# A fused attention and token-mixing kernel: band mask moved to TensorE, coarse rows carried through their own projections, two PSUM slot sizes, TensorE kept in traced order

## The chip, the cores and the metric

The kernel runs on one core of one Trainium2 chip. Times are device microseconds (us) of one execution. A span is the time from the first to the last instruction of one profiled execution. It lies about 2 us under the time of the same execution. PE is TensorE, DVE VectorE, ACT ScalarE, POOL GpSimd, SP the engine whose queue issues most of the DMAs.

The kernel before shows two levels in its runs, near 246 and near 250 us. Runs more than 1.5% above the fastest of the same kernel are called slow and are left out of every ratio.

The profile of the kernel before is of an execution of 249.87 us, on the upper level (1.6% above the fastest run, so slow by the rule above). No profile of the lower level was kept.

## The reference

```python
# q, k, v: 8 batches x 8 heads x 576 rows x 64, float32
out_d    = softmax_attention(mean4(q), mean4(k), mean4(v))   # 144 coarse rows per head
out_up   = np.repeat(out_d, 4, axis=2)                       # back to 576 rows
mask     = np.abs(pos[:, None] - pos[None, :]) < 4           # a band of 7
out_loc  = softmax_attention(q, k, v, masked with mask)
x        = (out_up + out_loc) as [8, 576, 512]
wq, wk   = x @ w_q, x @ w_k                                  # 64 wide each
W        = (wq @ wk.T) / 8
out      = np.maximum(W @ x, 0) @ w_out                      # [8, 576, 512]
```

## The kernel before

Each batch passes through four stages. `stage_cast` loads a batch and casts it on POOL. `stage_a` transposes q and k on PE, sums groups of four rows on POOL, computes the local scores in windows of 58 queries by 64 keys, takes exp on ACT, and averages v on PE. `stage_b` does the coarse attention and the local products, and builds x and its transpose. `stage_c` does the mixing. One iteration of the main loop merges `stage_c` of batch i-2, `stage_b` of i-1, `stage_a` of i and the cast of i+1. The parts that the change and the argument touch:

```python
ps2 = tile_pool(name="ps2", bufs=4, space=PSUM)        # four slots of two banks, for everything
# ... masks, averaging matrices P, selection matrices sel: some 70 small POOL instructions ...
merge([stage_cast(0)])                                  # traced behind all of them

def score(pr_):                                         # local scores of one or two windows
    for i, n in enumerate(pr_):
        for hl in range(NP):
            for p, c in ((0, 0), (1, 1), (0, 1), (1, 0)):
                nc.tensor.matmul(p_[64*c:64*c+64, p, o:o+w], kT[...], qT[...], start=True, stop=True, ...)
    nc.scalar.activation(E, p_, Exp, scale=s_local)
    for n, t_ in e_:                                    # the band mask, on DVE
        nc.vector.tensor_tensor(t_, t_, masks[n], op=mult)

def sums():                                             # groups of four rows, on POOL
    # 2 additions of 128x1152, one of 128x576, five small ones: 7.2 us in all

def vd():                                               # averages of v
    # 5 matmuls from v16 into pv; ACT copies vd0, DVE multiplies into vblk

def up(n):                                              # coarse rows added to x
    nc.tensor.matmul(pu[:, 0, :], sel[n], od, start=True, stop=True)
    nc.vector.tensor_tensor(x_, x_, pu[:, 0, :], op=add)

def wt():                                               # wT = [wq wk] transposed
    for i in range(2):
        for r in range(4):
            nc.tensor.matmul(p_[:, i, 0:320], wqk16[:, r, :], xT[:, r, 320*i:320*i+320], ...)
# m2: 5 matmuls wk x; mx(r): four evacuations with ReLU; og(i): output matmuls, evacuation, store
```

The softmax here doesn't subtract the row's maximum and nothing guards it: scores larger than these inputs give would overflow.

Of the kernel before, what the change touches and what calls it, by code (L numbers as in the profile page):

```python
# [17 lines left out]

@with_exitstack
def kernel(  # L20
# [10 lines left out]
    nc = tc.nc  # L31
    B, H, S, D = q.shape
    DM = H * D
# [20 lines left out]
    ps2 = ctx.enter_context(tc.tile_pool(name="ps2", bufs=4, space=bass.MemoryType.PSUM))  # L54

    def ps(dtype=FP32, name="ps"):
        return ps2.tile([128, 2, 512 if dtype == FP32 else 1024], dtype, name=name, tag="ps")

# [41 lines left out]
    masks = {}  # L100
    for n in (0, 1, 4):
        t_ = cst.tile([128, WQ[n]], FP16, name=f"mask{n}")
        nc.vector.memset(t_, 1.0)
        for c in range(2):
            h_, off = t_[64 * c:64 * c + 64], K0[2 * n + c] - Q0[2 * n + c]
            asel(h_, [[-1, WQ[n]]], ALU.is_ge, 0.0, off + 3, 1)
            asel(h_, [[1, WQ[n]]], ALU.is_ge, 0.0, 3 - off, -1)
        masks[n] = t_
    masks[2] = masks[3] = masks[1]


    P = []
    for n in range(NW):
        t_ = cst.tile([128, 32], FP16, name=f"P{n}")
        nc.vector.memset(t_, 0.0)
        mid = (K0[2 * n] + 64) // 4 - G0[n]
        for c, lo, hi in ((0, 0, mid), (1, mid, GN[n])):
            u_ = t_[64 * c:64 * c + 64, lo:hi]
            off = K0[2 * n + c] - 4 * (G0[n] + lo)
            nc.vector.memset(u_, 0.25)  # L120
            asel(u_, [[-4, hi - lo]], ALU.is_ge, 0.0, off, 1)
            asel(u_, [[4, hi - lo]], ALU.is_ge, 0.0, 3 - off, -1)
        P.append(t_)
    P4 = cst.tile([128, 4, 32], FP16, name="P4rep")
    nc.vector.tensor_copy(P4, _ap(P[4], 0, [[row(P[4]), 128], [0, 4], [1, 32]]))
    blk = cst.tile([128, 4], FP16, name="blk")
    nc.vector.memset(blk, 1.0)
    asel(blk, [[-32, 4]], ALU.is_ge, 0.0, 0, 1)
    asel(blk, [[32, 4]], ALU.is_ge, 0.0, 31, -1)


    GR = 116
    sel = []
    for n in range(NW):
        t_ = cst.tile([128, 2, 64], FP16, name=f"sel{n}")
        nc.vector.memset(t_, 0.0)
        for c in range(2):
            u_ = t_[:, c, 0:WQ[n]]
            off = Q0[2 * n + c] - (4 * GR if n == 4 else 0)
            nc.vector.memset(u_, 1.0)  # L140
            asel(u_, [[1, WQ[n]]], ALU.is_ge, 0.0, off, -4)
            asel(u_, [[-1, WQ[n]]], ALU.is_ge, 0.0, 3 - off, 4)
        sel.append(t_.rearrange("p c w -> p (c w)"))


    rows = cst.tile([128, 2], FP32, name="rows")
    nc.vector.memset(rows, 1.0)
    for c in range(2):
        for i, w in ((0, WQ[0]), (1, WQ[4])):
            asel(rows[64 * c:64 * c + 64, i:i + 1], [[0, 1]], ALU.is_ge, 0.0, w - 1, -1)  # L150


    kdS, E_S, vd0S, vblkS, od1S = [], [], [], [], []
    for i in range(2):
        t_ = cst.tile([128, NP, 160], FP16, name=f"kd_{i}")
        nc.vector.memset(t_, 0.0)
        kdS.append(t_)
        es = {}
        for pr_ in PAIRS:
            t_ = cst.tile([128, 2, len(pr_), NP, 64], FP16, name=f"E{pr_[0]}_{i}")  # L160
            nc.vector.memset(t_, 1.0)
            es[pr_] = t_
        E_S.append(es)
        t_ = cst.tile([128, H, 65], FP16, name=f"vd0_{i}")
        nc.vector.memset(t_, 1.0)
        for n in range(4):
            asel(t_[32 * n:32 * n + 32, :, 64], [[0, H]], ALU.is_ge, 0.0, GN[0] - 1, -1)
        vd0S.append(t_)
        t_ = cst.tile([128, 2, 4, 65], FP16, name=f"vblk_{i}")
        nc.vector.memset(t_, 0.0)  # L170
        o_ = t_[:, :, :, 64]
        nc.vector.memset(o_, 1.0)
        asel(o_, [[0, 2], [-32, 4]], ALU.is_ge, 0.0, 0, 1)
        asel(o_, [[0, 2], [32, 4]], ALU.is_ge, 0.0, GN[4] - 1, -1)
        vblkS.append(t_)
        t_ = cst.tile([128, DM], FP16, name=f"od1_{i}")
        nc.vector.memset(t_, 0.0)
        od1S.append(t_)

    nc.vector.tensor_copy(wqk16, w32)  # L180
    for i in range(2):
        nc.vector.tensor_copy(wo16[:, 2 * i:2 * i + 2], wo32[i])
# [3 lines left out]
    def stage_cast(b):  # L186
# [12 lines left out]
        def vv():  # L199
            v32 = g["in"][3]  # L200
            v16 = g["v16"] = big.tile([128, NW, H, 65], FP16, name="v16", tag="v16", bufs=3)
            nc.gpsimd.tensor_copy(v16[:, :, :, 0:64], v32)
            nc.gpsimd.memset(v16[:, :, :, 64:65], 1.0)
# [3 lines left out]
    def stage_a(b):  # L207
        g = st[b]

        def tr(key):  # L210
            def f_():
                t_ = g[key]
                p_ = g["p" + key] = ps(FP16, "p" + key)
                for j in range(NP):
                    for f in range(4):
                        o = (j % 2) * 512 + 128 * f
                        nc.tensor.transpose(p_[:, j // 2, o:o + 128],  # L217
                                            t_[:, f, 2 * j:2 * j + 2, :], id16)
# [9 lines left out]
        def rem():  # L228
            qT, kT = g["qT"], g["kT"]
            pr = ps(FP16, "pr")  # L230
            for j in range(NP):
                nc.tensor.transpose(pr[:, 0, 128 * j:128 * j + 128],
# [25 lines left out]
        def score(pr_):  # L258
            def f_():
# [4 lines left out]
                for i, n in enumerate(pr_):  # L264
                    for hl in range(NP):
                        for p, c in ((0, 0), (1, 1), (0, 1), (1, 0)):
                            m = 2 * n + c
                            o = i * W + hl * w
                            nc.tensor.matmul(p_[64 * c:64 * c + 64, p, o:o + w],  # L269
                                             kT[64 * p:64 * p + 64, hl, K0[m]:K0[m] + 64],  # L270
                                             qT[64 * p:64 * p + 64, hl, Q0[m]:Q0[m] + w],
                                             start=True, stop=True, tile_position=(64 * p, 64 * c))
# [5 lines left out]
                if pr_ == (1, 2):  # L278
                    e_ = [(1, E.rearrange("p a n h w -> p (a n h) w")[:, :, 0:w])]
                else:  # L280
                    e_ = [(n, E[:, :, i, :, 0:w]) for i, n in enumerate(pr_)]
                for n, t_ in e_:
                    m_ = masks[n]
                    bc = [[0, t_.shape[1]]] if len(t_.shape) == 3 else [[0, 2], [0, NP]]
                    nc.vector.tensor_tensor(t_, t_, _ap(m_, 0, [[row(m_), 128]] + bc + [[1, w]]),  # L285
                                            op=ALU.mult)
            return f_

        def vd():
            v16, vd0, vblk = g["v16"], vd0S[b % 2], vblkS[b % 2]  # L290
            pv = ps(name="pv")
            for n in range(4):
                nc.tensor.matmul(pv[32 * n:32 * n + 32, 0, :], P[n], v16[:, n, :, 0:64],
                                 start=True, stop=True, tile_position=(0, 32 * n))
            nc.tensor.matmul(pv[:, 1, :], P4.rearrange("p a t -> p (a t)"), v16[:, 4, :, 0:64],
# [12 lines left out]
    def stage_b(b):  # L308
        g = st[b]
        vd0, vblk, od1 = vd0S[b % 2], vblkS[b % 2], od1S[b % 2]  # L310
# [3 lines left out]
        def cs(i):  # L314
            def f_():
                kd, qd = kdS[b % 2], g["qd"]
                if i == 0:
                    g["Ec"] = big.tile([128, 2, 2, 2, T], FP16, name="Ec", tag="Ec")
                p_ = ps(name="pcs")
                for hh in range(2):  # L320
                    for p in range(2):
                        nc.tensor.matmul(p_[:, p, hh * T:(hh + 1) * T],  # L322
# [3 lines left out]
                nc.scalar.activation(g["Ec"][:, i].rearrange("p a c t -> p a (c t)"),  # L326
                                     p_[:, :, 0:2 * T], ACTF.Exp, scale=s_coarse)
            return f_

        def cr():  # L330
            kd, qd = kdS[b % 2], g["qd"]
            Er = g["Er"] = big.tile([128, 2, T], FP16, name="Er", tag="Er")
            p_ = ps(name="pcr")
            for hl in range(NP):
                for p in range(2):
                    nc.tensor.matmul(p_[32 * hl:32 * hl + 32, p, 0:T],
                                     kd[64 * p:64 * p + 64, hl, 128:160],
                                     qd[64 * p:64 * p + 64, hl, :],
                                     start=True, stop=True, tile_position=(64 * p, 32 * hl))
            nc.scalar.activation(Er, p_[:, :, 0:T], ACTF.Exp, scale=s_coarse)  # L340

        def ca(i):
            def f_():
                Ec, Er = g["Ec"], g["Er"]
                if i == 0:
                    g["od0"] = big.tile([128, DM], FP16, name="od0", tag="od0")
                    g["rc"] = big.tile([128, 2, 2, 4], FP32, name="rc", tag="rc")
                od, rc = (g["od0"], od1)[i], g["rc"]
                lo, hi = ((0, 128), (GR, T))[i]
                M = hi - lo  # L350
                p_ = ps(name="pca")
                for p in range(2):
                    nc.tensor.matmul(p_[0:M, p, 0:260], Er[:, p, lo:hi],  # L353
                                     vblk[:, p].rearrange("a h e -> a (h e)"),
                                     start=True, stop=False, skip_group_check=True)
                    for hl in range(NP):
                        nc.tensor.matmul(p_[0:M, p, 65 * hl:65 * hl + 65],  # L357
                                         Ec[:, hl // 2, p, hl % 2, lo:hi], vd0[:, 2 * hl + p, :],
# [7 lines left out]
            return f_  # L366

        def av(n):
            def f_():
# [6 lines left out]
                for s_ in range(2):  # L376
                    for hh in range(NP):
                        for c in range(2):
                            h = 4 * (s_ ^ c) + hh
                            nc.tensor.matmul(  # L380
# [12 lines left out]
        def up(n):  # L393
            def f_():
                x_ = g["x"][n]
                pu = ps(name="pu")
                nc.tensor.matmul(pu[:, 0, :], sel[n], od1 if n == 4 else g["od0"],
                                 start=True, stop=True)
                nc.vector.tensor_tensor(x_, x_, pu[:, 0, :], op=ALU.add)
            return f_  # L400
# [159 lines left out]
```

## Time and profile before

| | before |
|---|---|
| time, median of three runs | 246.19 us (245.99 to 250.73) |
| span of the profiled execution (249.87 us, upper level) | 248.1 us |
| start of the third batch's sums (filling) | 68.1 us |
| one iteration (see below) | 25.62 us |
| from the eighth batch's sums to the end (draining) | 52.3 us |

The sums of a batch are one easily found POOL instruction per iteration, so their starts serve as a clock. An iteration is a quarter of the time from the fourth batch's sums to the eighth's, by the timeline of POOL. Before the change these stand at 93.29 and 195.78 us.

From the page of the kernel before: first busy time and share of the span, then the busy share in 40 equal slices of the span, in tenths, and the clock that PE was granted.

```profile
PE 170.3 (69%) x2464; PEld 99.1 (40%) x2464; DVE 169.7 (68%) x328; ACT 105.3 (42%) x137; POOL 129.4 (52%) x179
PE   0007049347868779787778788778677887888692
DVE  6450828994599559965986489848993898596021
POOL 7898992992099309930894069605970491000000
PEclk9999657959999997999979979999999889999659
```

The filling shows at the left: PE does nothing until 18.1 us (the first three slices), while POOL is full, mostly with building constants. In the middle PE and DVE are both at 7 to 9 tenths, so neither looks like the limit. The clock falls to 0.5 to 0.7 in the filling and at the end, where PE has gaps; three slices in the middle show 0.7 as well.

The busy-time table by windows of the kernel before, for two iterations: stretch, length, busy time (and number of instructions) of PE, weight loads, DVE, ACT and POOL, then granted clock, DMA share and GB/s.

```profile
110.00:136.00 26.00, 20.70 (x314) 12.01 (x311) 19.27 (x34) 13.08 (x18) 14.22 (x13) 0.93 0.68 192
136.00:161.80 25.80, 20.95 (x313) 12.18 (x311) 19.92 (x34) 13.10 (x18) 14.23 (x13) 0.93 0.64 187
```

DVE is busy 20 of 26 us. What that hides is in the timeline of the same kernel (start, length, engine, line, operation, output and inputs, shapes, count, and what it waited for):

```profile
147.13 1.15 POOL L247 TENSOR_TENSOR qd<-sum_2410 128x576 f16<-128x576 f32 x1
147.97 0.57 DVE L285 TENSOR_TENSOR E_1_229<-E_1_229,mask_96 128x464 f16<-128x464 f16 x1 [0.39 <-ACT E_1_229 L274]
148.36 2.14 POOL L245 TENSOR_TENSOR sum_2413<-kT 128x1152 f32<-128x1152 f16 x1
148.46 2.30 DVE L285 TENSOR_TENSOR E_1_229<-E_1_229,mask_102 128x464 f16<-128x464 f16 x1
```

The same product of the same size took 0.57 us when POOL's short addition (`qd`) had 0.31 us left to run, and 2.30 us when POOL's large sum had started 0.1 us earlier. Both ended 0.26 us after that POOL instruction did, so most of the 2.30 us is waiting. The Trainium skill, "SBUF — State Buffer", section "SBUF: two separate sides", says that GpSimd and a VectorE operation with two SBUF inputs lock the same ports for a whole instruction. This trace agrees.

In the chain of waits (start, length, what; followed back from the last instruction) these products and the work queued behind them carry the second half of the iteration:

```profile
146.99 0.95 ACT E_1_229 L274
147.97 2.79 DVE E_1_229 L285 x2
...
153.39 1.71 DVE E_1_231 L285
...
155.70 1.40 DVE E_1_233 L285
...
157.83 1.13 DVE os L487
...
159.62 0.74 DVE xT L413
...
160.40 0.97 PE pw L429 x6
```

From the first mask product at 147.97 to the projections at 160.40 the chain never leaves DVE.

### The profile page before, as it was taken

The page shows a single profiled execution, that of the slowest core. Times are in us where ns is not written, and L with a number is a line of the kernel's source. Part 1 is how long each engine was busy: PE and PEld are TensorE (multiplying, and loading weights), DVE is VectorE, ACT ScalarE, POOL GpSimd, SP SyncE. Part 2 cuts the span into 40 slices and gives each one's busy share as a digit, 9 for nine tenths or more (in the row PEclk, how much of TensorE's full clock was granted, in tenths as well). Part 3 has the DMA queues.
Part 4 walks back from the last instruction along what each step waited for, and adds up shares of the span by engine and source line. Part 5 has one row for each costly group of instructions (what it writes and reads, how often), then busy time and mean ns, then how long its engine had stood idle before and what let it go on. Part 6 is the DMA issues. An engine that isn't in the chain of part 4 may idle for free.

```text
span 248.1 us, 5991 instructions
## 1 busy us (share of the span) xinstructions
PE 170.3 (69%) x2464; PEld 99.1 (40%) x2464; DVE 169.7 (68%) x328; ACT 105.3 (42%) x137; POOL 129.4 (52%) x179
## 2 busy tenths in 40 slices
PE   0007049347868779787778788778677887888692
PEld 0006026225534554354335544454335543544230
DVE  6450828994599559965986489848993898596021
ACT  2006336317543763376425653466356544430321
POOL 7898992992099309930894069605970491000000
PEclk9999657959999997999979979999999889999659
DMA  6989999897301995259744974299511021105005
GB/s 214 273 206 361 256 251 265 186 345 167 69 31 77 311 244 130 87 168 334 159 126 132 342 169 146 85 294 246 166 50 59 0 90 49 59 0 193 0 0 190
DMA packets 73947, 40.49 MB, mean 163 GB/s; under 512 B 52416, under 2 KB 68800, under 8 KB 73920
## 3 DMA queue, kind: packets, MB, share of 16 engines
q1 hardware_dynamic: 73920, 40.12, 55.3%
q8 instruction: 19, 0.31, 0.5%
q14 instruction: 8, 0.07, 0.1%
HBM read 30.67 MB, written 9.44 MB: 162 GB/s over the span
## 4 chain that ended last, share of the span: by engine, by line
DVE 34%; PE 32%; ACT 13%; SPq 9%; issue 6%; DMA 2%; POOL 2%; ACTq 0%; DVEq 0%
PE po L482 5%; DVE E_1_229 L285 5%; SPq L83 4%; DVE E_0_208 L285 4%; PE pw L429 3%; SPq L79 3%; DVE xT L413 3%; ACT qT L224 2%; ACT rmx L469 2%; DVE E_1_231 L285 2%; PE pmx L463 2%; DVE os L487 2%; PE pca L353 2%; DMA v_263<-in_v_dram 2%; ACT wk L442 1%
## 5 line engine op out<-in xcount | busy, mean ns | idle before, releaser
L482 PE MATMUL po<-wo_95,rmx 128*128 128x512 f16 x128 | 36.4, 437 | 0.2 <-ACT os L485 0.2
L482 PEld LDWEIGHTS <-rmx 128*128 128x128 f16 x128 | 13.3, 110 | 19.2 <-issue 9.3
L385 DVE RECIPROCAL rz<-pav 128x8 f32<-128x8 f32 x40 | 7.9, 198 | 17.1 <-PE pav L380 17.0
L471 DVE TENSOR_SCALAR rmx<-pmx 128x576 f16<-128x576 f32 x16 | 12.0, 748 | 7.3 <-PE pmx L465 7.3
L269 PE MATMUL psc<-qT,kT 64*64 64x58 f16 (+1 forms) x640 | 10.2, 202 | 9.5 <-DVE x_2027 L387 2.0
L485 ACT COPY os<-po 128x1024 f32<-128x1024 f32 x8 | 8.1, 1012 | 17.1 <-PE po L482 17.1
L360 DVE RECIPROCAL rc<-pca 128x8 f32<-128x8 f32 (+1 forms) x16 | 3.2, 201 | 16.8 <-PE pca L357 16.7
L429 PE MATMUL pw<-xT,wqk_94 128*128 128x320 f16 x64 | 11.4, 300 | 4.5 <-DVE vblk_220 L299 1.6
L217 PE MATMUL pq_278<-id_64,q_251 128*128 128x128 f16 x16 | 1.9, 312 | 18.1 <-POOL q_251 L195 18.1
L269 PEld LDWEIGHTS <-kT 64*64 64x64 f16 x640 | 7.7, 116 | 15.7 <-issue 4.7
L413 DVE COPY xT<-px 128x1280 f16<-128x1280 f16 x16 | 12.9, 814 | 1.2 <-PE px L411 1.2
L487 DVE COPY os<-po 128x1024 f32<-128x1024 f32 x8 | 9.7, 1214 | 5.9 <-PE po L482 5.9
L469 ACT ACTIVATE rmx<-pmx 128x576 f16<-128x576 f32 x16 | 10.4, 653 | 5.4 <-PE pmx L465 5.4
L499 ACT COPY ol<-pol 64x512 f32<-64x512 f32 x8 | 4.6, 579 | 16.1 <-PE pol L497 16.1
L326 ACT ACTIVATE Ec<-pcs 128x576 f16<-128x576 f32 x16 | 9.5, 649 | 2.5 <-PE pcs L322 2.5
L224 ACT COPY qT<-pq_278 128x2048 f16<-128x2048 f16 x1 | 1.9, 1866 | 18.0 <-PE pq_278 L217 18.0
L451 PEld LDWEIGHTS <-wk 128*64 128x64 f16 x40 | 4.0, 116 | 13.1 <-ACT wk L442 10.1
L285 DVE TENSOR_TENSOR E_1_229<-E_1_229,mask_102 128x464 f16<-128x464 f16 x4 | 9.2, 2302 | 0.0
L285 DVE TENSOR_TENSOR E_0_208<-E_0_208,mask_102 128x464 f16<-128x464 f16 x4 | 9.2, 2300 | 0.0
L217 PEld LDWEIGHTS <-q_251 128*128 128x128 f16 x16 | 1.6, 147 | 18.1 <-POOL q_251 L195 18.1
L432 ACT CAST wT<-pw 128x640 f16<-128x640 f32 x8 | 5.5, 692 | 7.3 <-PE pw L429 7.3
L429 PEld LDWEIGHTS <-wqk_94 128*128 128x128 f16 x64 | 5.5, 97 | 7.8 <-DVE vblk_220 L299 2.1
(615 smaller groups left out, 581.2 us busy)
## 6 DMA issues: line engine op xcount, KB each, us to landing
out_dram<-os SPq DMA_DIRECT2D x16, 512.0 KB, 2.9
v_72<-in_v_dram SPq DMA_DIRECT2D x10, 128.0 KB, 3.2
v_263<-in_v_dram SPq DMA_DIRECT2D x10, 128.0 KB, 3.4
v_445<-in_v_dram SPq DMA_DIRECT2D x10, 128.0 KB, 3.3
v_822<-in_v_dram SPq DMA_DIRECT2D x10, 128.0 KB, 3.2
v_1276<-in_v_dram SPq DMA_DIRECT2D x10, 128.0 KB, 3.2
v_1730<-in_v_dram SPq DMA_DIRECT2D x10, 128.0 KB, 3.3
v_2184<-in_v_dram SPq DMA_DIRECT2D x10, 128.0 KB, 4.2
```

The costliest lines, as they stand in the source:

```text
L83: nc.sync.dma_start(v32[64 * c:64 * c + 64, n], _ap(vb, K0[2 * n + c] * D, [[D, 64], [S * D, H], [1, D]]))
L269: nc.tensor.matmul(p_[64 * c:64 * c + 64, p, o:o + w], kT[64 * p:64 * p + 64, hl, K0[m]:K0[m] + 64], qT[64 * p:64 * p + 64, hl, Q0[m]:Q0[m ...
L285: nc.vector.tensor_tensor(t_, t_, _ap(m_, 0, [[row(m_), 128]] + bc + [[1, w]]), op=ALU.mult)
L326: nc.scalar.activation(g["Ec"][:, i].rearrange("p a c t -> p a (c t)"), p_[:, :, 0:2 * T], ACTF.Exp, scale=s_coarse)
L385: nc.vector.reciprocal(rz[:, n], _ap(p_, 64, [[row(p_), 128], [512, 2], [65, 4]]))
L413: nc.vector.tensor_copy(g["xT"][:, 2 * i:2 * i + 2, :], p_[:, :, 0:640])
L429: nc.tensor.matmul(p_[:, i, 0:320], wqk16[:, r, :], xT[:, r, 320 * i:320 * i + 320], start=(r == 0), stop=(r == 3))
L469: nc.scalar.activation(d_, s_, ACTF.Relu)
L471: nc.vector.tensor_scalar_max(d_, s_, 0.0)
L482: nc.tensor.matmul(p_[:, ff, :], rmx[:, r, c:c + 128], wo16[:, r, :], start=(r == 0), stop=(r == 3))
L485: nc.scalar.copy(os_, p_)
L487: nc.vector.tensor_copy(os_, p_)
```

## The change

The intent has five parts. The band mask becomes a matmul: a constant of 0 and -60000 is accumulated into the score's PSUM slot ahead of the scores, so that exp gives zero. The coarse rows are no longer upsampled and added to x. They are transposed (`odT`), projected by themselves and accumulated with the projections of the local part, and they enter M2 through summed keys (`wd`). PSUM is split into three slots of two banks and two of one bank. TensorE instructions keep the order in which they are traced. And most of POOL's constants are gone or traced behind the first cast.

```diff
-    ps2 = ... tile_pool(name="ps2", bufs=4, space=PSUM)
+    ps2 = ... tile_pool(name="ps2", bufs=3, space=PSUM)
+    ps1 = ... tile_pool(name="ps1", bufs=2, space=PSUM)       # one bank: pr, pod, pwk, pwd, pm2, pmr, pol
+    TEN_ = _InOrder(tc, nc.tensor)        # every call: tc.keep_in_program_order(...)
     def score(pr_):
+                for i, n in enumerate(pr_):
+                    for p in range(2):
+                        TEN_.matmul(p_[:, p, i * W:(i + 1) * W], neg[64*p:64*p+64, ...],
+                                    _ap(id16, ..., [[row(id16), 64], [0, NP], [1, w]]),
+                                    start=(i == 0), stop=False, skip_group_check=True)
-                for n, t_ in e_:
-                    nc.vector.tensor_tensor(t_, t_, masks[n], op=ALU.mult)
-        def up(n): ...
+        def odt():
+            for r in range(4):
+                for od, lo, hi in ((g["od0"], 0, 128), (g["od1"], 128, T)):
+                    TEN_.transpose(p_[:, r * T + lo:r * T + hi], od[:, 128*r:128*r+128], id16[...])
+            nc.vector.tensor_copy(odT, ...)
     def wt():
+                for r in range(4):
+                    TEN_.matmul(p_[:, i, 0:288], wqk16[:, r, :],
+                                _ap(odT, r*T + 72*i, [[row(odT), 128], [1, 72], [0, 4]]), ...)
+        def wks(): ...                     # 8 small matmuls: keys summed in fours
     def m2():
+            TEN_.matmul(p_[0:64], wd[:, 0], g["od0"], start=True, stop=False)
+            TEN_.matmul(p_[0:64], wd[0:16, 1], g["od1"], start=False, stop=False)
-        (mx: four evacuations of 128x576)
+        (mx: two of 128x1024, one of 128x256 for the remaining rows)
+    merge([stage_cast(0)])                 # now ahead of most constants
# ... cut: xT without padding, wT in two fixed buffers, v16 in three, weights of the merge ...
```

## The prediction

> **What bounds the kernel now.** After filling (0 to 58 us) come six iterations of 25.2 to 26 us (58 to 213 us), then a drain of 35 us. The busy-time table by windows gives, for 136.0-161.8 us: PE 20.95, DVE 19.9, POOL 14.2, ACT 13.1 us. In the chain of waits DVE holds 34% of the span, PE 32%, ACT 13%. In the second half of each iteration DVE runs without a gap for 13 us (148 to 160 us in the timeline).
>
> The DVE queue is inflated by the mask products. The timeline has them at 0.57 us [...] and 2.30 us where the same 128x464 product meets POOL's sums. The Trainium skill, "SBUF — State Buffer", section "SBUF: two separate sides", calls the VectorE/GpSimd pair an exclusive lock, held for a whole instruction, also by a VectorE operation with two SBUF inputs; this trace agrees.
>
> **What the change removes, per batch.** Mask products, 0.57+2.30+1.79+1.47 = 6.1 us of DVE. Five coarse-row adds of 0.67 us (3.4) and their five 512-column matmuls (about 1.1 us of PE). DVE: 19.9 to about 12 us, with an odT copy (0.5) added. ACT stays near 13, POOL near 14.
>
> **What it adds.** 36 more TensorE pairs per batch: 10 mask matmuls (232 columns, about 0.1 us each, some side by side), 8 projections of odT (0.12 each), 2 more into M2 (0.22), 21 small ones. From start-to-start times in the trace (8 matmuls of 512 columns in 1.9 us) I estimate PE's streaming work at 16.3 us before and 17.9 after. PE is in order and has three large PSUM slots for four.
>
> **Critical path.** What remains once DVE is relieved: (a) wT evacuation, qT evacuation (1.87), wk, wd, then M2 on ACT in a row, with PE short of other work: 1.5-2.5 us of stall; (b) a POOL loop: sums need qT/kT with the remainder rows, sums take 7.2 us, the v cast 2.3, and only then the v downsampling matmuls, in order, may run: about 10.6 us from remainder transposes to them, while PE has some 7.2 us of work between. Remainder to remainder: 10.6 + about 11.7 = 22.3 us, perhaps 21, against 25.7 now. So 5-6 iterations gain about 3.5-4.5 us each: about 20 us. Filling: POOL builds constants until 16.2 us although q lands by 6; with the cast first, the first q transpose moves from 18.1 to about 8.5, but the remainder cast waits behind 18 constant instructions, and the second batch's loads land no earlier (24-36 us). I expect 5 us at the first v cast and about 10 us by the third batch's remainder transposes, 67 to about 57. Drain: 2-4 us shorter while batch 7 is still in, its last 22 us unchanged.
>
> **Prediction: 212 us, range 201 to 225.** Chances: faster by over 2% 0.96, within 2% 0.03, slower 0.01.
>
> **What would show it.** Iterations of 21-22.5 us in steady state; DVE near 12 us of each; PE busy 85-90% of an iteration and its largest waits on ACT (wk, wd, M2, psc evacuation) and on the POOL v cast; first transpose near 8.5 us; granted clock at or above 0.91 on average.
>
> **What would make it wrong.** In-order PE blocked at the head of its queue by three-slot PSUM recycling (iteration of 24 us: about 224). Or the v cast hidden and the ACT chain overlapped (20 us: 201). DMA at 0.64 of an iteration now would reach 0.8. Mask matmuls with a repeated moving operand could stream slower than I count.

## The result and the profile after

The changed kernel takes 227.28 us in the median of four runs (227.06 to 227.52). The kernel before took 248.46 in its four (245.99 to 252.32). The ratio of the fast runs is 0.9236, with a 95% interval of 0.9214 to 0.9258. Ratios are the mean time of one kernel's fast runs over that of the other's of the same rounds, so not quite the ratio of the medians. The fast runs alone are 246.1 us before and 227.3 after, so 18.8 us were gained. Faster was right, but 227.3 lies above the predicted range.

The page of the kernel after:

```profile
PE 180.7 (80%) x2752; PEld 112.2 (50%) x2752; DVE 104.3 (46%) x262; ACT 103.1 (46%) x137; POOL 115.9 (51%) x131
PE   0336077759988998899898989898989998999681
DVE  6005046523466337354726472646364546477022
POOL 3587991993079607970698059904990393000000
PEclk9999999857999999999999999999999999999999
```

DVE fell from 169.7 to 104.3 us and PE rose from 170.3 to 180.7. PE now starts in the second slice. The busy-time table by windows, for the end of the filling and one iteration:

```profile
36.00:62.00 26.00, 20.93 (x345) 14.18 (x345) 11.12 (x31) 12.16 (x16) 13.57 (x12) 0.80 0.97 238
109.05:132.11 23.06, 21.51 (x350) 13.34 (x350) 12.07 (x30) 12.67 (x18) 13.57 (x13) 1.00 0.81 211
```

The iteration took 23.06 us, and PE has records for 21.5 us of it. In the iteration that starts at 132.11 the timeline of PE marks four waits, 1.36 us in all:

```profile
133.38 0.38 PE L27 MATMUL psc<-id_67,neg 64*128 64x232 f16 x4 [0.34 <-DVE rmx L445]
134.39 1.90 PE L27 MATMUL po<-wo_98,rmx 128*128 128x512 f16 x8 [0.25 <-DVE x_2457 L350]
141.73 0.38 PE L27 MATMUL pv<-v_2_140,P_149 128*32 128x512 f16 x1 [0.57 <-POOL v_2_140 L163]
144.85 0.67 PE L27 MATMUL pw<-odT,wqk_97 128*128 128x288 f16 x4 [0.20 <-DVE xT L368]
```

That looks like a kernel bound by PE. The experiments show that it is not quite so. The span splits like this, by the starts of the sums:

| us | before | predicted | after |
|---|---|---|---|
| to the third batch's sums | 68.1 | about 58 | 62.9 |
| five iterations | 127.7 | about 20 less | 115.3 |
| from the eighth batch's sums to the end | 52.3 | 2 to 4 less | 47.0 |
| span | 248.1 | 32 to 34 less | 225.2 |

The difference of 22.9 us is 5.2 in the filling, 12.4 in the iterations and 5.3 in the draining. About 4 of the 22.9 are the upper level of the profile before (18.8 us in fast runs), and no trace says in which stage they lie. So each of the three parts may be too large.

The chain of waits of the kernel after, one iteration:

```profile
109.07 1.20 DVE rmx L445
...
111.33 1.90 PE po L27 x8
113.22 0.99 PE pod L27 x8
...
115.15 1.83 PE po L27 x8
...
117.44 0.68 PE px L27 x10
...
118.14 0.65 DVE xT L368
...
119.09 1.13 DVE os L470
120.22 0.66 DVE vblk_197 L258 x2
120.88 0.56 DVE xT L368
...
121.79 2.13 PE pw L27 x16
...
126.94 1.07 PE pk_2379 L27 x16
...
128.09 1.87 ACT kT L184
...
129.96 0.60 ACT M_2396 L429
...
131.21 0.34 PE pr L27 x4
```

It runs from DVE's ReLU through both halves of the output matmuls, the coarse transposes and the xT copies to the projections, and on through the kT and M evacuations. There are three stretches on DVE or ACT: 2.3 us from the ReLU to the first output matmul, 3.65 us of evacuations between px and pw, and 2.5 us for kT and M. In each of them PE has other work for most of the time, so PE stays busy while the chain runs elsewhere.

### The profile page after: what moved, and what is told of

It is laid out like the page before. It is cut to its first block, busy times and chain, and to the rows that moved or that the text cites. A ratio compares the mean times of both kernels' runs of the same rounds, so it can differ in the third digit from the quotient of the medians.

```text
span 225.2 us, 6421 instructions
## 1 busy us (share of the span) xinstructions
PE 180.7 (80%) x2752; PEld 112.2 (50%) x2752; DVE 104.3 (46%) x262; ACT 103.1 (46%) x137; POOL 115.9 (51%) x131
## 4 chain that ended last, share of the span: by engine, by line
PE 49%; DVE 17%; POOL 16%; ACT 10%; issue 3%; DMA 3%; POOLq 0%; DVEq 0%; ACTq 0%
PE po L27 11%; PE pw L27 8%; ACT kT L184 5%; DVE xT L368 5%; DVE rmx L445 4%; PE pav L27 3%; PE pmx L27 3%; PE pod L27 3%; DMA q_72<-in_q_dram 3%; PE psc L27 3%; DVE os L470 3%; PE px L27 2%; PE pca L27 2%; POOL qd L207 2%; PE pwd L27 1%
## 5 line engine op out<-in xcount | busy, mean ns | idle before, releaser
L27 PE MATMUL po<-wo_98,rmx 128*128 128x512 f16 x128 | 30.4, 380 | 2.3 <-ACT rmx L443 0.6
L27 PEld LDWEIGHTS <-rmx 128*128 128x128 f16 (+1 forms) x160 | 14.1, 100 | 18.1 <-ACT rmx L443 0.7
L368 DVE COPY xT<-px 128x928 f16<-128x928 f16 (+1 forms) x32 | 14.3, 453 | 11.4 <-PE px L27 11.0
L27 PEld LDWEIGHTS <-wqk_97 128*128 128x128 f16 x128 | 12.2, 100 | 6.5 <-DVE xT L368 2.9
L468 ACT COPY os<-po 128x1024 f32<-128x1024 f32 x8 | 8.1, 1012 | 11.8 <-PE po L27 10.6
L445 DVE TENSOR_SCALAR rmx<-pmx 128x1024 f16<-128x1024 f32 x8 | 9.8, 1224 | 7.3 <-PE pmx L27 7.3
L27 PE MATMUL pw<-odT,wqk_97 128*128 128x288 f16 x64 | 11.0, 297 | 1.5 <-DVE xT L368 1.5
L443 ACT ACTIVATE rmx<-pmx 128x1024 f16<-128x1024 f32 x8 | 8.2, 1024 | 5.9 <-PE pmx L27 5.9
L27 PE MATMUL pw<-xT,wqk_97 128*128 128x288 f16 x64 | 10.8, 293 | 0.0
L27 PE MATMUL psc<-id_67,neg 64*128 64x232 f16 (+1 forms) x80 | 8.7, 280 | 2.1 <-DVE rmx L445 2.1
L27 PE MATMUL pol<-wo_98,rmx 128*64 128x512 f16 x32 | 8.4, 385 | 0.0
```

The lines of the kernel that those rows point to most:

```text
L27: return lambda *a, **k: self._tc.keep_in_program_order(f_(*a, **k))
L368: nc.vector.tensor_copy(g["xT"][:, 2 * i:2 * i + 2, o:o + m * w].rearrange("p r (m w) -> p r m w", m=m), p_[:, :, lo:lo + 64 * m].rearrang ...
L443: nc.scalar.activation(d_, p_, ACTF.Relu)
L445: nc.vector.tensor_scalar_max(d_, p_, 0.0)
L468: nc.scalar.copy(os_, p_)
```

## The experiments

Three theories for the missing 15 us. **A**: PE's own stream of matmuls is the bound, and I counted it too low. **B**: the fixed order or the three large slots block PE. **C**, formed after the second group of runs: two loops of nearly the same length run side by side through the iteration, and I had priced one of them.

All kernels gave correct results. Iterations are measured as above, in the profile of each run; the profile was of a fast run except for before_pe_mask and for the kernel before (see above).

| run | edit | time, median (lowest to highest) | third sums | iteration |
|---|---|---|---|---|
| before | | 248.46 (245.99 to 252.32) | 68.1 | 25.62, upper level |
| after | | 227.28 (227.06 to 227.52) | 62.9 | 23.06 |
| free_order | scheduler orders PE | 228.23 (228.09 to 228.64) | 62.8 | 23.49 |
| slots_as_before | four large slots | 228.62 (228.41 to 228.94) | 61.3 | 23.26 |
| dve_mask | mask on DVE again | 235.47 (233.32 to 238.49) | 62.5 | 24.18 |
| before_pe_mask | before, mask on PE | 234.17 (229.98 to 235.19) | 64.1 | 23.63, slow |
| mask_twice | mask matmuls doubled | 230.92 (228.43 to 233.61) | 62.2 | 23.47 |
| pod_sorted | coarse transposes sorted | 226.46 (226.04 to 227.47) | 62.7 | 22.99 |
| v_early | v cast ahead of sums | 225.28 (223.83 to 227.81) | 60.1 | 23.07 |
| rows_added | coarse rows on DVE again | 251.06 (249.40 to 251.62) | 68.6 | 26.15 |
| both_loops | v_early and pod_sorted | 222.62 (221.26 to 223.44) | 61.5 | 22.49 |
| both_os_act | and an evacuation to ACT | 218.18 (217.83 to 218.68) | 60.9 | 22.13 |
| const_first | constants before the cast | 225.51 (223.55 to 226.96) | 59.3 | 23.07 |
| rows_added_free | rows_added, old slots and order | 233.05 (230.76 to 235.75) | 66.1 | 23.67 |
| weights_late | weight loads later | 228.12 (227.75 to 228.76) | 63.6 | 23.10 |
| all_four | both_os_act, batch 1's v later | 217.91 (217.38 to 219.69) | 59.1 | 22.14 |
| all_four_wlate | and weight loads later | 218.50 (217.40 to 220.36) | 60.1 | 22.09 |

### Order and slots (free_order, slots_as_before)

```diff
-    TEN_ = _InOrder(tc, nc.tensor)
+    TEN_ = nc.tensor
```

> The changed kernel with the scheduler free to order TensorE again (it moves about 5% of the matmuls). The changed kernel takes 227.3 us, with 23.06 us an iteration, PE busy 21.5 of it. Theory A (PE's own issue of its matmuls costs more than I counted, about 20.9 us of every iteration): same matmuls, so 225 to 230 us, iteration 22.8 to 23.3. Theory B (PE blocked at the head of its queue by the fixed order): iteration near 21.5 to 22, about 215 us.

```diff
-    ps2 = ... bufs=3 ... ; ps1 = ... bufs=2 ...
+    ps2 = ... bufs=4 ...                          # psm() takes half of such a slot
```

> The changed kernel with four large PSUM slots shared by everything, as before the change, in place of three large and two small. Theory A: PE bound, 226 to 231 us. Theory B (three large slots are too few and stall an in-order PE): the extra large slot gives back the waits for the mask slot and for the output slot, about 0.8 us of an iteration or 6 us in all, so 221 us; but small tiles then also take large slots, so it could as well lose some us.

Both are within 0.6% of the changed kernel, and both are a little slower: by 0.4 and 0.2 us an iteration in their traces. Neither gives anything back, so theory B falls for each of the two alone. Both together were not tried on the changed kernel. The figure of 5% of the matmuls in the expectation was not checked by a run.

### The mask, from both sides (dve_mask, before_pe_mask)

```diff
# dve_mask: the changed kernel
-                        TEN_.matmul(p_[:, p, i * W:(i + 1) * W], neg[...], id16 repeated, ...)
+                for n, t_ in e_:
+                    nc.vector.tensor_tensor(t_, t_, masks[n], op=ALU.mult)
# before_pe_mask: the kernel before, the same edit the other way round
```

> The changed kernel with the band mask multiplied by VectorE again. DVE per iteration 12.1 -> about 18 us (products of 0.6 to 2.3 us where POOL is busy), PE about 0.9 us less. If the mask products are the cause of the old bound: iteration 24.5 to 25.5, 238 to 248 us. Theory A (PE stream is the bound, DVE has slack): at most 2% slower, 223 to 231 us.

> The kernel before with the band mask by TensorE alone, everything else (order, slots, coarse rows, constants first) as before. DVE per iteration 19.9 -> about 13.5 us, PE +0.9. I expect most of the gain per iteration from this: iteration 25.6 -> 23.3 to 24, ratio to the kernel before 0.93 to 0.95, about 229 to 234 us. If the gain needs the in-order queue or the slots: ratio above 0.97.

In the kernel before, the mask on PE alone gives a ratio of 0.9334 (0.914 to 0.9528), most of the gain. (The interval is wide because three of the five fast runs before were near 250 us in these rounds; against the two near 246.4 us the ratio is 0.94.) Its profile fell in the slow state, so its iteration of 23.63 us is only rough. Taken back out of the changed kernel, the mask costs 7.5 us between fast runs, and 1.1 us of each iteration, though it puts several microseconds back on DVE (16.9 us in an iteration of dve_mask, against 12.1 us after). The two numbers need not agree, because removing work helps only until the next chain is longer. dve_mask came out slower than pure theory A allowed (at most 231 us): DVE has less slack than its 12 of 23 us suggest.

### Is PE the bound? (mask_twice, pod_sorted)

```diff
-                    for p in range(2):
+                    for p in (0, 1, 0, 1):       # each mask matmul twice; start only for the first
```

> The changed kernel with each of its ten mask matmuls issued twice (the result stays right, the sum only gets more negative). In the changed kernel four of them take 0.31 us from start to start, so PE gets about 0.82 us more work in an iteration. Theory A (PE stream is the bound): iteration 23.06 -> 23.7 to 23.9, total +5 to +7 us, 232 to 234 us. Rivals (PE waits for slots, ACT, POOL; extra PE work fits in its waits): under +2 us.

This run decides nothing between A and C. The times have two levels here, 228.4 and 233.5 us, so only the trace is used. There the mask groups of an iteration take 1.30 us from start to start in place of 0.81. So 0.49 us of PE work was added, not the 0.82 us expected. The iteration grew by 0.41 us in the mean of four, and by 0.30 in three of them. The groups also stand in the chain that runs through the output matmuls, so C asks for growth too.

```diff
-            for r in range(4):
-                for od, lo, hi in ((g["od0"], 0, 128), (g["od1"], 128, T)):
+            for od, lo, hi in ((g["od0"], 0, 128), (g["od1"], 128, T)):
+                for r in range(4):
```

> The changed kernel with its eight coarse transposes in another order: the four of 128 rows, then the four of 16 rows, in place of alternating. The alternating group takes 1.09 us from the first start to the next group's, of which I had counted 0.3. If alternating row counts costs (weights of the next not loaded under the running one): group 0.5 to 0.7 us, iteration -0.4 to -0.5 by theory A, total -3 to -4 us, 223 to 224 us. If each small matmul has a fixed cost: group stays at 1.0 to 1.1, no change.

From the first transpose to the next group is 0.51 us here (by the timeline, 112.79 to 113.30) in place of 1.09; in the chains of the kernel after and of both_loops the eight pieces take 0.99 and 0.41 us. So alternating between 128 and 16 rows did cost some 0.58 us. Yet the iteration stayed at 22.99 us. Theory A does not allow this: PE records fell from 21.5 to 20.9 us of an iteration, and the iteration did not. The chain of waits of pod_sorted, from the middle of the sums on, shows why:

```profile
115.03 0.72 POOL kd L210 x2
...
116.08 2.27 POOL v L163
...
118.39 0.74 PE pv L27 x5
...
119.78 0.76 DVE vblk L258 x2
...
121.44 2.13 PE pw L27 x16
...
131.76 2.10 POOL sum L205
```

PE now reaches the v downsampling earlier and waits 1.14 us there for POOL's v cast, against 0.57 us before. The chain has moved to the loop that I had predicted: remainder transposes, sums, v cast, downsampling, projections, kT, M, remainder transposes. The view itself goes back from 115.03 us to a load of v that landed at 114.86. But by its timeline POOL runs without a gap from the start of the sums at 108.77 us through the v cast, so that load held nothing up.

### Two loops (v_early, both_loops, both_os_act)

v_early keeps POOL in traced order with the v cast of a batch ahead of its sums. It also has the constants ahead of the first cast, which const_first tests alone.

```diff
-            nc.gpsimd.tensor_copy(v16[:, :, :, 0:64], v32)      # and the other POOL casts and sums
+            POO_.tensor_copy(v16[:, :, :, 0:64], v32)           # POO_ = _InOrder(tc, nc.gpsimd)
-        return [(1, qk), (1, vv)]
+        return [(1.1, lambda: None), (.1, qk), (.8, vv)]        # casts behind the sums of the batch before
-    merge([stage_cast(0)])                                      # moved behind the constants; v of batch 0
+    stage_cast(0)[1][1]()                                       # behind its sums
```

> The changed kernel with GpSimd kept in traced order so that the v cast of a batch runs before that batch's sums, not after them. This takes away the wait of the v downsampling matmuls on the v cast (0.57 us an iteration in the trace, and the loop remainder transposes - sums - v cast - downsampling of 10.6 us that I predicted). If that loop is what sets 23.06 us: iteration -0.6 us or more, total 221 to 223 us. Theory A, pure: PE would still wait less by 0.57 us, unless it then waits for the next thing (xT copies, output slot): 222 to 227 us.

PE no longer waits for a v cast in any of the four iterations, and they still take 23.07 us. The chain of that run passes through the same groups as that of the kernel after, through pod and the xT copies. So neither edit moves the iteration alone. Theory C says that together they must.

> The v cast ahead of the sums and the sorted coarse transposes together. Alone, neither moved the iteration (23.06 and 22.98 us against 23.06). Theory C: two loops of almost the same length run side by side. One goes remainder transposes - sums - v cast - downsampling - projections - kT and M evacuation - remainder transposes (over POOL); the other goes output matmuls - coarse transposes - scores - xT copies - projections - kT and M evacuation - ReLU - output matmuls (over PE, DVE, ACT). Each change shortens one of them, so both together must show what neither shows alone: iteration 22.4 to 22.6 us, total 1.5 to 3 us under the v cast alone, 221 to 223 us. Theory A (PE stream alone): the sorted transposes would have helped alone, so nothing new here, 23.0 us.

The iteration is 22.49 us, and all four iterations agree to 0.02 us. This is a 2x2 design with times of 23.06, 23.07, 22.99 and 22.49 us. The gain exists only in the corner where both loops are shorter. The next edit takes the output evacuation out of the chain of the second loop:

```diff
-                if i == 0:
-                    nc.scalar.copy(os_, p_)
-                else:
-                    nc.vector.tensor_copy(os_, p_)
+                nc.scalar.copy(os_, p_)
```

> The same with the second output evacuation (1.13 us on DVE, standing between the two xT copies in the chain) given to ACT. Theory C: the second loop loses 0.4 to 1.1 us more: iteration 21.5 to 22.1, total 217 to 220 us. If PE's own stream of about 20.9 us less 0.5 is near: not under 21 us.

From the chain of waits of both_loops, the two places concerned (the second stands between the xT copies, and is gone from both_os_act's chain):

```profile
87.60 0.41 PE pod L27 x8
...
92.88 1.13 DVE os L471
```

The iteration falls to 22.13 us, just above the 21.5 to 22.1 expected, and the time to 218.18 us. In both_os_act PE has records for 21.02 of 22.13 us, and waits for about 0.9 us of an iteration, so what remains is closer to theory A than before.

### The filling (const_first, weights_late, all_four, all_four_wlate)

```diff
-    merge([stage_cast(0)])
     P = {}                       # and the other constants
     ...
+    merge([stage_cast(0)])
     for i in range(B + 2):
```

> The changed kernel with its remaining GpSimd constants traced ahead of the first cast again (they fit in POOL's 4 us of waiting for q). First sums 18.94 -> 15 us, first v cast ends 29.1 -> 23.6. If the filling is priced by POOL work alone, as I predicted: third sums 62.9 -> 57 us, total -5.5 us, 222 us. If it is the loop through PE and the loads of the second batch (v lands at 38 us): second sums about 36, third sums 60 to 61, total -2 to -3 us, 224.5 to 225.5 us. Iteration unchanged, 23.06.

The first sums start at 15.3 in place of 18.9 us and the third at 59.3 in place of 62.9. Of the 4.9 us that the changed kernel lost against the predicted 58, 3.6 come from there: POOL waited 4.0 us for q with nothing to do, then ran 24 constant instructions (the prediction counted 18) while the remainder cast stood behind them. v_early's gain in time (225.28 us) is this one (225.51 us); its own edit is worth nothing alone.

```diff
     st[0]["in"] = load(0)
+    st[1]["in"] = load(1)        # ahead of the loads of w_q, w_k and w_out; taken out of the loop
```

> The changed kernel with the weight loads issued after the second batch's loads, so that these land about 4 us earlier (v at about 34 in place of 38 us). If late landing sets the filling: third sums 62.9 -> 59 to 60, total -3 us. If the loop through POOL and PE sets it (in the chain of the changed kernel no transfer stands between 6 and 63 us): third sums within 0.5 us of 62.9 and total 226.5 to 228 us.

The second batch's last v load is issued by 29.5 us in place of 33.8. The third sums do not come earlier (63.6 us), nor does the end (228.12 us). So in the changed kernel the landing of the second batch is not what the filling waits for. Its chain of waits from the first v cast on shows the loop instead:

```profile
26.81 2.27 POOL v_0_136 L163
...
32.40 1.84 PE pq_459 L27 x16
...
37.88 0.34 PE pr L27 x4
...
38.71 2.11 POOL sum_582 L205
...
46.03 2.27 POOL v_1_138 L163
...
48.34 1.17 PE pv L27 x5
...
51.83 2.92 PE pw L27 x16
...
62.02 0.33 PE pr L27 x4
...
62.93 2.10 POOL sum_1023 L205
```

The loop is the same as in the middle, and some of its PE parts run slowly: 16 transposes in 1.84 us against 1.00 us later, pw in 2.92 against 2.13. The Trainium skill, "TensorE: Matmul & The Clock Gate", Part 1, says that the array runs at half its clock by default and after an idle window of about 3.4 us. There are two slow stretches. The first agrees: from the first transposes (1.89 us for 16, at 8.59 us) to about 35 us PE works at about half its later rate, with waits of up to 7.9 us in between. The clock that the profile reports does not show it, though: it stands at 1.00 there. In the second stretch, from about 43 to 53 us, the reported clock is 0.50, but PE had stood idle for only 1.1 us before it, so a window of idleness of that length is not what this trace shows. Over the chain the low rate adds about 2.5 us, an estimate: 0.43 for each of two pv groups, 0.84 for pq, 0.79 for pw, by the durations of the same groups later in this trace. No run took the low rate away by itself.

```diff
# all_four, on top of both_os_act; all_four_wlate adds the edit of weights_late
-            m_.append(stage_cast(i + 1))
+            m_.append(stage_cast(i + 1) if i else stage_cast(1)[:2] + [(.8, lambda: None)])
+        if i == 1:               # v of batch 1 lands late: cast it behind that batch's sums
+            m_.append([(1.08, lambda: None), (.01, stage_cast(1)[2][1]), (.9, lambda: None)])
```

> v cast early from batch 2 on, batch 1's v after its sums, constants first, sorted transposes, both output evacuations on ACT. Against both_os_act (218.2 us, second sums 40.9, third 60.9): second sums 35 us, third sums 57 to 59, iteration 22.13 as there, total 215 to 217 us. If the landing of v (38 us) and of batch 2 (q 39, k 43, v 54) sets the third sums: still 60 to 61, 218 us.

> all_four with the weight loads after the second batch's. If landing matters once the loop is gone: third sums 3 us earlier than in all_four, 212 to 215 us. If the loop is all: equal to all_four within 1 us.

In all_four the v cast of batch 1 goes behind its sums and the second sums start at 34.9 us; the third still start at 59.1. Its time is equal to both_os_act within noise, against 215 to 217 us expected. Earlier landing on top gave nothing, 218.5 us. What keeps the third sums at 59 to 60 us in all these variants stays open: the loop of this stretch is there again in all_four's chain, with the granted clock at 0.84 between 35 and 57 us.

all_four is the best version measured: 217.91 us, ratio 0.8801 (0.8719 to 0.8884) to the kernel before; both_os_act cannot be told from it.

### The coarse rows (rows_added, rows_added_free)

```diff
+        def up(n): pu = sel[n] @ od0 (n == 4: and sel5 @ od1); x += pu        # five a batch, on PE and DVE
-        odt, wks, the odT half of wt, the two wd matmuls of m2
```

> The changed kernel with the coarse rows upsampled by a matmul and added on VectorE again, as before the change (own projections, coarse transposes and summing matmuls gone; the mask stays with TensorE). Per iteration PE loses about 1.0 (projections) + 1.1 (coarse transposes) + 0.5 (summing) + 0.6 (M2) and gains about 1.3 (upsampling), DVE gains 3.4 and loses 0.5: PE 21.5 -> about 19.7, DVE 12.1 -> 15. Theory A: iteration 21.7 to 22.5, so 5 x 0.6 to 1.4 us faster, less about 3 us for twelve more constants on GpSimd at the start: 219 to 226 us. If the relief of DVE by this part was needed: iteration above 23.3, 230 us or more.

This miss was large: 251 us where I expected 219 to 226. In its trace PE waits about 1.5 us per iteration at a small slot behind DVE's queue and 1.4 us for ACT's copy of the keys (`wk`), the iteration is 26.15 us, and the granted clock falls to 0.87 in the iteration from 147 us (0.90 over four).

> The coarse rows upsampled and added on DVE as in rows_added, but with four large slots and the scheduler's order as before the change. In rows_added the upsampling matmuls and the ReLU of the rest shared two small slots with long DVE queues (PE waited 1.5 us an iteration) and the clock fell to 0.87. If that was the reason for 251 us: 231 to 236 us, iteration 23.7 to 24.3, as in the kernel before with the PE mask (234 us). If adding the rows on DVE itself costs that much: 245 us or more.

With the old slots and the scheduler's order the same work takes 233.05 us in the median (231.0 in its two fast runs), and 23.67 us an iteration. Which of the two matters was not separated. So the slots and the order, which give nothing back in the changed kernel, are not neutral for every variant of it. Against free_order (228.3 us, which differs in the slots too) the separate projections are worth some 2.7 us between fast runs, and mostly elsewhere than intended: the third sums start 3.3 us earlier without the selection constants on POOL, the five iterations gain 1.9 us, and the draining loses 2.5 us (47.03 against 44.55 us), presumably because the last batches' chain runs through the added PE work (argued, not shown). My expectation that the projections cost time in a PE-bound loop was wrong in the iterations and right in the draining.

## Why the prediction was wrong, point by point

- **Direction, and DVE's relief: right.** DVE per iteration was predicted at about 12 us and measured at 12.07. POOL was predicted near 14 and measured 13.57, ACT near 13 and measured 12.67. First q transpose predicted at about 8.5, measured 8.59. First v cast predicted 5 us earlier; it ended at 29.1 against 33.7.
- **"about 10.6 us from remainder transposes" to the v downsampling: right**, 10.59 us in the trace (131.14 to 141.73). **"about 11.7" for the way back: too small**, 12.47 us (141.73 to 154.20). That makes 23.06 in place of 22.3.
- **"while PE has some 7.2 us of work between", and with it "perhaps 21": the step that failed.** In the 10.59 us from remainder transposes to the downsampling PE waits for only 1.16 us, so it has 9.4 us of work there, not 7.2. I took the POOL loop as the only limit and allowed that better overlap would beat it. v_early took its wait away and the iteration did not move, because a second loop through the output matmuls, the DVE queue and the projections is just as long. both_loops showed it.
- **"1.5-2.5 us of stall" on ACT (wT, qT, wk, wd, M2): did not come.** Between 86 and 178 us the list of PE's waits in the changed kernel has none on ACT. They are on DVE and on the v cast, 1.4 us an iteration in all.
- **"5-6 iterations gain about 3.5-4.5 us each: about 20 us": failed.** They gained 2.56 us each, 12.4 in five. Even my own 22.3 against 25.7 gives only 3.4, so the sum was also more generous than its parts. The 2.56 us are themselves measured against the upper level of the kernel before.
- **212 as a total: about 4 us too low by its own parts.** They were read from the trace of an execution of 249.87 us and add up to 32 to 34 us, which gives 216 to 218. To 212 they lead only from the median of 246.19 us. No mechanism hangs on this.
- **"I estimate PE's streaming work at ... 17.9 after": too low** to say how close PE is to full. PE has records for 21.5 us of each iteration. (Records count the overlap of matmuls differently from the estimate: before the change they gave 20.9 us where it had 16.3. But PE waits only 1.4 us of 23.06.) One part was measured: the eight alternating transposes took 0.99 us, of which 0.58 is due to their order. But this was not what set the time (pod_sorted).
- **"about 10 us by the third batch's remainder transposes": failed**, 5.2 us (with the upper level of the kernel before in it). I priced the filling by POOL's work and the loads. const_first gave 3.6 us back; the rest is the same loop through PE at a low rate (argued from the chain, not shown by a run). weights_late excludes the landing of the loads in the changed kernel.
- **"Drain: 2-4 us shorter": too small**, 5.3 us, with the same reserve.
- **Warnings.** In-order blocking and three-slot recycling cost nothing that giving back the order or the slots would have returned (free_order, slots_as_before). The DMA share of an iteration rose to 0.81 as said and cost nothing that the runs show. The granted clock is 0.975, above 0.91 as predicted, and PE is busy 93% of an iteration where I expected 85 to 90%.

## What to carry to other kernels

When an engine is relieved, look for all loops that are about as long as the new iteration, not for the one the chain of waits prints: the chain shows one loop, and an edit that shortens it by half a microsecond can move the chain and leave the time. Two edits that each do nothing should be tried together before either is dropped. In this kernel the move from DVE to PE that paid was that of products that waited for POOL's instructions (2.30 us for one of 128x464), and the constants were best built while POOL waited for its first load (3.6 us).

## What the Trainium skill lacked or had wrong

- "TensorE: Matmul & The Clock Gate", Part 2, LDWEIGHTS: it gives the time of a weight load by its columns, and no page has a time for a sequence that alternates between stationary operands of 128 and of 16 rows. Eight such transposes took 0.99 us alternating and 0.41 us when sorted by rows. Why is not shown.
- The same page, Part 4 (PE-mode transpose): it gives about 275 to 390 ns for a 128x128 transpose. That is the duration of one; Part 4 has no start-to-start time for a group of transposes. Here sixteen back to back took 1.00 us, 0.06 us each, and 1.84 us at the low rate of the filling, so for sizing a group its start-to-start time is the one to use.
- "Perfetto Trace Analysis", section "Optimization Strategies", advises to optimize the engines "that are blocking the critical path". It does not say that two loops of equal length can hide each other: 23.06, 23.07 and 22.99 us with none or either shortened, 22.49 with both.
